# One PSUM pool for both forms of the first layer, a third chunk in float32, and the splits on GpSimd

## The chip, the cores and the metric

The kernel runs on one core of one Trainium2 chip. The metric is the device time of one execution in microseconds (us), lower is better. TensorE (PE in the profile; PEld is its weight load) multiplies matrices into PSUM, which has eight banks of 128 x 512 float32; VectorE (DVE), ScalarE (ACT) and GpSimd (POOL) work on elements, and GpSimd's operations here read and write SBUF alone; SyncE (SP) issues most DMA transfers.

## The reference

A Fourier mixing of 8 sequences of 3008 tokens of width 256, followed by a two-layer network with a hard-swish:

```python
X = np.fft.fft(x, axis=1)            # x: (8, 3008, 256) float32
X = np.fft.fft(X, axis=2).real       # bridge: (24064, 256)
h = X @ w_in                         # (256, 2048)
g = h * np.clip(h + 3.0, 0.0, 6.0) / 6.0
out = g @ w_out                      # (2048, 256)
```

## The kernel before

**Steps.** The batches are taken in four pairs p. Each pair has 12 chunks ck of 256 moving columns (the last is smaller), and each chunk goes through the 2048 hidden features in 8 blocks fc of 256. One (p, ck, fc) is a step s, 384 in all; a chunk is 8 steps. Below, "step 12" is s = 12, and "chunk 3" is the fourth chunk of the first pair, steps 24 to 31. The program runs with an order written out by hand: each engine takes its instructions in program order. In step s TensorE does the second layer for step s (`mlp2`, line 733, seven products per block, 14 matmul instructions of 256 columns; the float32 product is two instructions each) and the first layer for step s + 2.

**First layer, direct form** (`mlp1`, from `mlp1_products` and `activate`): tiles u and v are two float32 products (line 570, four instructions each); VectorE makes s (line 579), u (586) and v (588); ScalarE makes two relus (682); VectorE makes two gates (685), and these are the last readers of u's and v's banks. It is used for the steps below `SPLIT`, plus two, that is for chunks 0 and 1.

**First layer, split form** (`even_half`, `odd_half`, `other_sign`, `first_gate`, `second_gate`): u is still a float32 product (623), issued a step ahead; the product with the other half of the weights is made of six single-pass matmuls of a rounded type (639) from operands that are split in three parts: KW for the weights and k for the columns q. The split of KW is made once, by `split_w`, in four pieces of 512 columns in steps 8 to 11; k is made once per chunk by `split_q`. Both call `split` (605 on ScalarE, 607 and 608 on VectorE), and `split_w` adds two ScalarE scalings (615, 616). In each split-form step ScalarE copies tile y from v (644) ahead of the relu.

**Recombination.** GpSimd makes three sums per step (`combine`, line 699) that are the operands of four of the seven products; once per chunk, when its last block is done, it recombines the products (`finish`, in the first step of the next chunk), and VectorE transposes them for the store.

**Around the steps.** `beside(p)` puts work beside the steps: `ahead` runs at the start of a step, `middle_fns` in it, `behind` after the first part of `mlp2` (or inside `odd_half`). For the next pair of batches GpSimd loads and folds inputs (`load_x`, `fold`; for the second half of the first pair `load_half`, `fold_half`), TensorE does a first-stage unit (`stage1`, line 291; `stage1_quarters`, 395 and 398, in steps 8, 10, 15 and 18), whose two banks ScalarE copies out (302, 402), and a second stage (519, or 480 in steps 8, 16 and every 8 steps on), whose bank ScalarE copies into q (522, 483). Of the 24 units of `stage1`, eight belong to each later pair.

**PSUM.** Four banks hold the second layer's sums (`ps_a`). The other four are, up to step 13, pool `ps_d` (one bank, tag d) and pool `ps_h` (three banks in rotation, tag uv); in step 13 (`SPLIT - 1`) `close_ps` closes both and opens `ps_u` with four single banks a0, a1, y0 and y1. In the split form the step's parity picks the tags: u takes a, v takes y. A first-stage unit in step s takes y and a of parity s + 3; the even half of chunk step s + 3 comes right after part of `mlp2` and takes the same a. `stage1` copies first the y bank, then the a bank:

```python
ps = [bank([P, 2, D], "ps1"), other_bank([P, 2, D], "ps1")]
...
for b in range(2):
    nc.scalar.copy(z[:, b], ps[b][0:PB + PZ])
```

Of the kernel before, what the change touches and what calls it, by code (L numbers as in the profile page):

```python
# [60 lines left out]
def kernel(  # L61
# [10 lines left out]
    nc = tc.nc  # L72
# [38 lines left out]
    dctx = tc.tile_pool(name="ps_d", bufs=1, space=PSUM)  # L111
    ps_d = dctx.__enter__()
    hctx = tc.tile_pool(name="ps_h", bufs=3, space=PSUM)
    ps_h = hctx.__enter__()
    ps_u = None

    x_r = x.rearrange("b (r n) d -> (b r) (n d)", n=XC)
    x_pn = x.rearrange("b (n1 n2) d -> (b n1) n2 d", n2=N2)
# [151 lines left out]
    def bank(shape, name):  # L270
        if starting[0]:
            return ps_a.tile(shape, F32, tag="acc", name=name)
        if ps_u is not None:
            return ps_u.tile(shape, F32, tag=f"y{turn_of[0] % 2}", name=name)
        return ps_d.tile(shape, F32, tag="d", name=name)

    def other_bank(shape, name):
        if ps_u is not None:
            return ps_u.tile(shape, F32, tag=f"a{turn_of[0] % 2}", name=name)
        return ps_h.tile(shape, F32, tag="uv", name=name)  # L280

    def stage1(pr, c):
        y = pr.y[c]
        ps = [bank([P, 2, D], "ps1"), other_bank([P, 2, D], "ps1")]
        for h in range(2):
            last = (c, h) == (NXC - 1, 1)
            for b in range(2):
                n = 1 if last else 2  # L290
                nc.tensor.matmul(ps[b][h * PB:(h + 1) * PB, 0:n], F[rows(b), 0:PB], y[rows(b), 2 * h:2 * h + n],  # L291
                                 start=True, stop=not last, skip_group_check=last)


            cosine, sine = slice(0, P + 1), slice(P + 1, D)
            for k, (j, cs) in enumerate([(XC - 1, cosine), (XC, cosine), (XC - 1, sine), (XC, sine)] if last else ()):
                for b in range(2):
                    nc.tensor.matmul(ps[b][h * PB:(h + 1) * PB, 1, cs], table(k + 1, b), y[rows(b), j, cs],
                                     start=False, stop=(k % 2 == 1), skip_group_check=True)
        z = zpool.tile([PB + PZ, 2, 2, D], F32, tag="z", name="z")  # L300
        for b in range(2):
            nc.scalar.copy(z[:, b], ps[b][0:PB + PZ])  # L302
# [17 lines left out]

    def first_banks(m):
        if not middle:
            middle.extend(ps_h.tile([P, NM, 2, 1], F32, tag="uv", name="pt") for h in range(2))
        return [bank([P, 2, D], "ps1") for h in range(2)], [t[:, m] for t in middle]

    def quarters(m, part):
# [59 lines left out]
    def stage1_quarters(hb, m):  # L386
# [14 lines left out]
        for h in range(2):  # L401
            nc.scalar.copy(z[:, h], ps[h][0:PX])
# [156 lines left out]

    def mlp1_products(ch, fc, between=None):  # L560
        of, nq, q = ch.ck % 2 * TB, ch.nq, ch.pr.q[ch.ck // 2]
        u = ps_h.tile([P, 2, TB], F32, tag="uv", name="u")
        v = ps_h.tile([P, 2, TB], F32, tag="uv", name="v")
        for blk, ps in ((0, u), (1, v)):
            if blk and between:
                between()
            r = slice(0, P - blk)
            for i in range(2):
                f = 2 * fc + i
                nc.tensor.matmul(ps[:, i, 0:nq], W1[r, blk, f * P:(f + 1) * P], q[r, blk, of:of + nq],  # L570
                                 start=True, stop=True)
        return u, v

    def activate(ch, fc, u, v, between=None):
        of, nq, qn = ch.ck % 2 * TB, ch.nq, ch.pr.qn[ch.ck // 2]
        s = spool.tile([P, 2, TB], F32, tag="s", name="s")
        for i in range(2):
            f = 2 * fc + i
            nc.vector.scalar_tensor_tensor(s[:, i, 0:nq], qn[:, of:of + nq], WN[:, f:f + 1], u[:, i, 0:nq],  # L579
                                           op0=AL.mult, op1=AL.add)  # L580
# [5 lines left out]
        nc.vector.scalar_tensor_tensor(u[:], s[:], 1.0, v[:], op0=AL.mult, op1=AL.add)  # L586
        relu(t[:, 0], u[:], 1.0 / 6.0)
        nc.vector.scalar_tensor_tensor(v[:], s[:], -1.0, v[:], op0=AL.mult, op1=AL.add)
# [15 lines left out]
    def split(high, low, rest, x):  # L604
        nc.scalar.mul(high, x, 1.0 - EPS / 2.0)
        h = high.bitcast(F32)
        nc.vector.tensor_tensor(low, x, h, op=AL.subtract)
        nc.vector.scalar_tensor_tensor(rest, h, 1.0 + EPS, x, op0=AL.mult, op1=AL.subtract)

    def split_w(i):  # L610

        cs = slice(i * WB, (i + 1) * WB)
        low, rest = (spool.tile([P, WB], F32, tag="s", name="part") for j in range(2))
        split(KW[:, 0, cs], low[:], rest[:], W1[:, 1, cs])
        nc.scalar.mul(KW[:, 1, cs], low[:], 1.0 / EPS)
        nc.scalar.mul(KW[:, 2, cs], rest[:], -1.0 / EPS)
# [16 lines left out]
    def odd_half(ch, fc, step, between):  # L633
# [8 lines left out]
        t = spool.tile([P, 2, 2, TB], F32, tag="t", name="t")  # L642
        un, vn, yn, tn = u[:, :, 0:nq], v[:, :, 0:nq], y[:, :, 0:nq], t[:, :, :, 0:nq]
        nc.scalar.copy(yn, vn)  # L644
        between()
        nc.vector.scalar_tensor_tensor(un, un, 1.0 + EPS, yn, op0=AL.mult, op1=AL.add)  # L646
        relu(tn[:, 0], un, 1.0 / 6.0)
        ch.front[fc] = [u, v, t, s]

    def other_sign(ch, fc):  # L650
# [196 lines left out]
    def exponent_b(j):  # L847
        pm = [PM[j % len(PM)][:, i].bitcast(F16) for i in range(2)]
        if j in (0, 1, 4):
            exs[j] = ps_h.tile([P, WB], F32, tag="uv", name="ex")[:]  # L850
        elif j in (2, 5):
            exs[j] = ps_d.tile([P, WB], F32, tag="d", name="ex")[:]
        elif j % 2 == 0:
            exs[j] = bank([P, WB], "ex")[:]
        else:
# [80 lines left out]
        nc.sync.dma_start(out=F[:, 0:5 * PB], in_=c_stage1[:, 8 * PB:13 * PB])  # L936

    def keep_awake(n, w=2 * TB):
        ps = ps_d.tile([P, 2 * TB], F32, tag="d", name="awake")
# [6 lines left out]
    awake = ps_d.tile([P, TB // 4], F32, tag="d", name="awake")  # L946
# [133 lines left out]
    def beside(p):  # L1080
# [72 lines left out]
    def close_ps():  # L1153
        nonlocal ps_u
        hctx.__exit__(None, None, None)
        dctx.__exit__(None, None, None)
        ps_u = ctx.enter_context(tc.tile_pool(name="ps_u", bufs=1, space=PSUM))
# [103 lines left out]
    def run(fns, t):  # L1261
        for f, a in fns.get(t, ()):
            f(*a)

    prev = None
    for s, (p, ck, fc) in enumerate(steps):
        if ck == 0 and fc == 0:
# [12 lines left out]
        else:  # L1280
# [9 lines left out]
            if s < SPLIT:  # L1290
                run(middle_fns, t)
                mlp1(*chunk(s + 2))
                if s == SPLIT - 1:
                    close_ps()
                    split_q(chunk(s + 3)[0])
                    even_half(*chunk(s + 3), s + 3)
                make_combine()
                mlp2(*chunk(s), 0)
                run(behind, t)
                mlp2(*chunk(s), 1)  # L1300
            else:
# [12 lines left out]
                mlp2(*chunk(s), 1, 1 + (t in behind))  # L1314
# [107 lines left out]
```

## Time and profile before

| | |
|---|---|
| median of 3 runs | 1901.78 us (1900.34 to 1902.53) |
| the profiled execution | 1902.44 us, span 1900.4 us |
| mean granted clock of TensorE in it | 0.997 |
| busy: TensorE, VectorE, GpSimd, ScalarE | 99%, 79%, 77%, 49% |

A line of the timeline has the start in us, the busy time in us, the engine, the line of the kernel, the operation, output <- inputs, shapes, how many instructions were merged, and in brackets the idle time before it with what ended it. A line of a group has the total busy time in us, the mean of one instruction in ns, and the idle time before. A line of a table of waits has the waiting engine and line, what it waited for, the total in us, how often, and the longest. Matmul ends are modelled, so that lengths of matmul groups are best read from start to start.

### The profile page before, as it was taken

How to read it: one execution, taken by the hardware profiler on the slowest of the kernel's cores; microseconds unless marked ns; L12 is line 12 of the kernel's file. 1: busy time of each engine (PE TensorE's matmuls, PEld its weight loads, DVE VectorE, ACT ScalarE, POOL GpSimd, SP SyncE). 2: the span in 40 equal slices, each digit the busy share in tenths (PEclk: the TensorE clock that was granted, in tenths of full speed). 3: DMA queues.
4: the chain of work that ended last, by engine and by line, in shares of the span. 5: the costliest groups of instructions: out<-in, count | busy, mean ns of one | idle time of the engine just before them, and what ended most of it. 6: DMA issues, size and time to landing. Idle time of an engine off the chain costs nothing.

```text
span 1900.4 us, 30550 instructions
## 1 busy us (share of the span) xinstructions
PE 1873.6 (99%) x10192; PEld 1642.0 (86%) x10192; DVE 1505.1 (79%) x2856; ACT 931.4 (49%) x1591; POOL 1457.0 (77%) x1658
## 2 busy tenths in 40 slices
PE   9989999999999999999999999999999999999998
PEld 6668888888988888888998888888899898999988
DVE  8977777777887777777887777777778887887887
ACT  6545444445445444454454444544454444444443
POOL 5676889887778887888768878888767667666775
PEclk9989999999999999999999999999999999999999
DMA  7432233311112223221112221222101101111011
GB/s 266 109 92 59 70 75 104 87 48 47 48 32 68 56 64 79 54 67 36 40 39 57 66 69 45 67 56 61 48 23 35 42 14 38 37 26 40 17 23 21
DMA packets 157378, 110.40 MB, mean 58 GB/s; under 512 B 122095, under 2 KB 135898, under 8 KB 157222
## 3 DMA queue, kind: packets, MB, share of 16 engines
q1 hardware_dynamic: 144966, 71.24, 14.9%
q0 software_dynamic: 11008, 36.63, 6.7%
q8 instruction: 81, 1.33, 0.3%
q10 hardware_dynamic: 1248, 0.59, 0.1%
q14 instruction: 75, 0.61, 0.1%
HBM read 71.93 MB, written 36.79 MB: 57 GB/s over the span
## 4 chain that ended last, share of the span: by engine, by line
PE 91%; DVE 4%; ACT 2%; issue 2%; POOL 1%; DMA 0%; DVEq 0%; ACTq 0%; POOLq 0%
PE acc L733 55%; PE u L623 16%; PE u L639 9%; PE v L639 4%; PE ps L519 2%; PE ps L291 1%; ACT z L302 1%; DVE a L685 1%; ACT t L682 1%; PE acc L709 1%; DVE s L579 0%; DVE s L629 0%; DVE u L586 0%; PE ps L356 0%; PE v L570 0%
## 5 line engine op out<-in xcount | busy, mean ns | idle before, releaser
L699 POOL TENSOR_TENSOR c<-a 128x512 f32<-128x512 f32 (+1 forms) x375 | 473.1, 1262 | 322.7 <-DVE a L685 269.8
L733 PE MATMUL acc<-c,G 128*128 128x256 f32 (+1 forms) x3008 | 701.0, 376 | 0.4 <-POOL c L699 0.2
L733 PEld LDWEIGHTS acc<-c,G 128*128 128x128 f32 x3008 | 566.6, 191 | 75.3 <-POOL c L699 3.4
L733 PE MATMUL acc<-a,G 128*128 128x256 f32 (+1 forms) x2256 | 603.6, 377 | 0.0
L733 PEld LDWEIGHTS acc<-a,G 128*128 128x128 f32 x2256 | 395.5, 190 | 53.8 <-issue 15.9
L629 DVE SCALAR_TENSOR_TENSOR s<-qn,WS,u 128x256 f32<-128x256 f32 (+1 forms) x736 | 315.9, 470 | 156.3 <-PE u L623 156.0
L682 ACT ACTIVATE t<-v,half 128x512 f32<-128x512 f32 (+1 forms) x384 | 260.7, 679 | 353.3 <-DVE v L653 350.2
L682 ACT ACTIVATE t<-u,half 128x512 f32<-128x512 f32 (+1 forms) x384 | 260.1, 677 | 353.5 <-DVE u L646 321.8
L623 PE MATMUL u<-q,W 128*128 128x256 f32 (+1 forms) x1472 | 374.3, 377 | 6.3 <-DVE a L685 3.1
L646 DVE SCALAR_TENSOR_TENSOR u<-u,y 128x512 f32<-128x512 f32 (+1 forms) x368 | 250.4, 680 | 154.8 <-ACT y L644 152.3
L623 PEld LDWEIGHTS u<-q,W 128*128 128x128 f32 x1472 | 274.2, 190 | 52.2 <-ACT z L302 12.3
L685 DVE SCALAR_TENSOR_TENSOR a<-t,v 128x512 f32<-128x512 f32 (+1 forms) x480 | 265.9, 571 | 57.9 <-ACT t L682 55.6
L644 ACT COPY y<-v 128x512 f32<-128x512 f32 (+1 forms) x368 | 213.7, 581 | 176.6 <-PE v L639 174.9
L699 POOL TENSOR_TENSOR c<-c,a 128x256 f32<-128x256 f32 (+1 forms) x375 | 271.9, 725 | 29.4
L699 POOL TENSOR_TENSOR c<-a,c 128x256 f32<-128x256 f32 (+1 forms) x375 | 270.5, 721 | 29.4
L685 DVE SCALAR_TENSOR_TENSOR a<-t,u 128x512 f32<-128x512 f32 (+2 forms) x448 | 261.3, 595 | 2.9 <-ACT t L682 2.9
L653 DVE SCALAR_TENSOR_TENSOR v<-s,u 128x512 f32<-128x512 f32 (+1 forms) x368 | 250.0, 679 | 1.3 <-ACT t L682 0.7
L639 PE MATMUL u<-k,KW 128*128 128x256 f32 (+1 forms) x1472 | 231.6, 279 | 1.8 <-DVE s L629 1.8
L639 PE MATMUL v<-k,KW 128*128 128x256 f32 (+1 forms) x736 | 214.0, 372 | 0.0
L639 PEld LDWEIGHTS u<-k,KW 128*128 128x128 f32 x1472 | 198.4, 188 | 2.4 <-ACT t L682 2.4
L639 PEld LDWEIGHTS v<-k,KW 128*128 128x128 f32 x736 | 139.0, 190 | 17.5
L699 POOL TENSOR_TENSOR r<-w,e 128x256 f32<-128x256 f32 (+1 forms) x92 | 88.9, 987 | 3.6
(147 smaller groups left out, 1179.0 us busy)
## 6 DMA issues: line engine op xcount, KB each, us to landing
out_dram<-o SPq DMA_DIRECT2D x744, 32.0 KB
T<-in_c_stage_dram SPq DMA_DIRECT2D x26, 512.0 KB
g<-zd SPq DMA_DIRECT2D x42, 256.0 KB
zd<-z SPq DMA_DIRECT2D x48, 192.0 KB
xt<-in_x_dram POOLq DMA_DIRECT2D x21, 256.0 KB
qn<-qd SPq DMA_DIRECT2D x16, 256.0 KB
st<-in_moe_w_out_dram POOLq DMA_DIRECT2D x7, 512.0 KB
xt<-in_x_dram POOLq DMA_DIRECT2D x17, 192.0 KB
```

The costliest lines, as they stand in the source:

```text
L291: nc.tensor.matmul(ps[b][h * PB:(h + 1) * PB, 0:n], F[rows(b), 0:PB], y[rows(b), 2 * h:2 * h + n], start=True, stop=not last, skip_group_c ...
L519: nc.tensor.matmul(ps[:, blk, u * P:n].rearrange("p (b k) -> p b k", b=2), g[:, kk, blk * (P + 1):blk * (P + 1) + P], T[gr][:, :, blk, kk, ...
L623: nc.tensor.matmul(u[:, i, 0:nq], W1[:, 0, f * P:(f + 1) * P], q[:, 0, of:of + nq], start=(i == 0), stop=True, skip_group_check=True)
L629: nc.vector.scalar_tensor_tensor(s[:, i, 0:nq], qn[:, of:of + nq], WS1[:, f:f + 1], u[:, i, 0:nq], op0=AL.mult, op1=AL.add)
L639: nc.tensor.matmul(o[:, i, 0:nq], KW[:, j, fs], ch.k[:, j, 0:nq], start=(j == 2 and i == 0), stop=True, skip_group_check=True)
L644: nc.scalar.copy(yn, vn)
L646: nc.vector.scalar_tensor_tensor(un, un, 1.0 + EPS, yn, op0=AL.mult, op1=AL.add)
L653: nc.vector.scalar_tensor_tensor(vn, sn, -2.0 * (1.0 + EPS), un, op0=AL.mult, op1=AL.add)
L682: nc.scalar.activation(t, h, AF.Relu, bias=half[:], scale=scale)
L685: nc.vector.scalar_tensor_tensor(dst, t, 1.0, h, op0=AL.min, op1=AL.mult)
L699: (eng or nc.gpsimd).tensor_tensor(out, in0, in1, op=AL.add)
L733: nc.tensor.matmul(ch.acc[i // 2][:, i % 2, 0:ch.n], G[:, i, fc, :], mv, start=(fc == 0 and i % 2 == 0), stop=(fc == NF - 1), skip_group_c ...
```

## The change

1. `ps_u` is opened at the beginning with its four tags, and no pool is closed. Up to the switch, a0 stands for the former `ps_d` (`lone_tile`), and a1, y0 and y1 are taken in rotation for the former `ps_h` (`ring_tile`).
2. `SPLIT` goes from 14 to 22: chunk 2 has the direct form too (its s uses the scaled row WS1, and `back` undoes the scale), and the split form begins with chunk 3. At the switch, three products of `mlp2` come ahead of `odd_half`.
3. `split_w` makes eight pieces of 256 columns, one in every second step from 8 to 22. In `split` VectorE's two operations become two of GpSimd and one of ScalarE; the pieces have a tag of their own.
4. `split_q` is called at the end of the step five steps ahead of its chunk, not four, and goes through the same `split`.
5. `stage1` and `stage1_quarters` copy the a bank (`ps[1]`) first, then hand back control (`yield`); in `odd_half` the VectorE operation on u and the relu are issued there, and only then the copy of the y bank with the transfers that follow it.

```diff
+    ps_u = ctx.enter_context(tc.tile_pool(name="ps_u", bufs=1, space=PSUM))
+    RING = ("a1", "y0", "y1")
+    ring = [0]
+
+    def ring_tile(shape, name):
+        ring[0] += 1
+        return ps_u.tile(shape, F32, tag=RING[(ring[0] - 1) % 3], name=name)
+
+    def lone_tile(shape, name):
+        return ps_u.tile(shape, F32, tag="a0", name=name)
...
         z = zpool.tile([PB + PZ, 2, 2, D], F32, tag="z", name="z")
-        for b in range(2):
-            nc.scalar.copy(z[:, b], ps[b][0:PB + PZ])
+        nc.scalar.copy(z[:, 1], ps[1][0:PB + PZ])
+        yield
+        nc.scalar.copy(z[:, 0], ps[0][0:PB + PZ])
...
         of, nq, qn = ch.ck % 2 * TB, ch.nq, ch.pr.qn[ch.ck // 2]
+        wn, back = (WN, 1.0) if ch.ck < 2 else (WS1, 1.0 + EPS)
...
     def split(high, low, rest, x):
         nc.scalar.mul(high, x, 1.0 - EPS / 2.0)
         h = high.bitcast(F32)
-        nc.vector.tensor_tensor(low, x, h, op=AL.subtract)
-        nc.vector.scalar_tensor_tensor(rest, h, 1.0 + EPS, x, op0=AL.mult, op1=AL.subtract)
+        nc.gpsimd.tensor_tensor(low, x, h, op=AL.subtract)
+        nc.scalar.mul(rest, h, EPS)
+        nc.gpsimd.tensor_tensor(rest, rest, low, op=AL.subtract)

     def split_w(i):

-        cs = slice(i * WB, (i + 1) * WB)
-        low, rest = (spool.tile([P, WB], F32, tag="s", name="part") for j in range(2))
+        cs = slice(i * TB, (i + 1) * TB)
+        low, rest = (spool.tile([P, TB], F32, tag="part", name="part") for j in range(2))
         split(KW[:, 0, cs], low[:], rest[:], W1[:, 1, cs])
         nc.scalar.mul(KW[:, 1, cs], low[:], 1.0 / EPS)
         nc.scalar.mul(KW[:, 2, cs], rest[:], -1.0 / EPS)
...
         nc.scalar.copy(yn, vn)
-        between()
+        late = between()
         nc.vector.scalar_tensor_tensor(un, un, 1.0 + EPS, yn, op0=AL.mult, op1=AL.add)
         relu(tn[:, 0], un, 1.0 / 6.0)
+        finish_parts(late)
...
-            for i in range(FF // WB):
-                put(NF + i, split_w, i)
+            for i in range(NF):
+                put(NF + 2 * i, split_w, i)
...
-    SPLIT = 2 * NF - 2
+    SPLIT = 3 * NF - 2
...
             if s < SPLIT:
                 run(middle_fns, t)
                 mlp1(*chunk(s + 2))
-                if s == SPLIT - 1:
-                    close_ps()
-                    split_q(chunk(s + 3)[0])
-                    even_half(*chunk(s + 3), s + 3)
                 make_combine()
                 mlp2(*chunk(s), 0)
-                run(behind, t)
+                if s == SPLIT - 1:
+                    even_half(*chunk(s + 3), s + 3)
+                finish_parts(begin_parts(t))
                 mlp2(*chunk(s), 1)
             else:
                 turn_of[0] = s + 3
+                n = 3 if s == SPLIT else 1 + (t in behind)
+                if s == SPLIT:
+                    mlp2(*chunk(s), 0, n)
                 if s + 2 < len(steps):
-                    odd_half(*chunk(s + 2), s + 2, lambda: run(behind, t))
-                mlp2(*chunk(s), 0, 1 + (t in behind))
+                    odd_half(*chunk(s + 2), s + 2, lambda: begin_parts(t))
+                if s > SPLIT:
+                    mlp2(*chunk(s), 0, n)
...
-                if s + 4 < len(steps) and (s + 4) % NF == 0:
-                    split_q(chunk(s + 4)[0])
+            if s > SPLIT - 6 and s + 5 < len(steps) and (s + 5) % NF == 0:
+                split_q(chunk(s + 5)[0])
```

More of the change, by code (lines that the diff above doesn't have):

```diff
@@ L110 @@
     ps_a = ctx.enter_context(tc.tile_pool(name="ps_a", bufs=4, space=PSUM))
[L111 to L115, printed above, removed]
+    ps_u = ctx.enter_context(tc.tile_pool(name="ps_u", bufs=1, space=PSUM))
[6 more added lines that the diff above has]
+        return ps_u.tile(shape, F32, tag="a0", name=name)
     x_r = x.rearrange("b (r n) d -> (b r) (n d)", n=XC)
@@ L272, in bank @@
             return ps_a.tile(shape, F32, tag="acc", name=name)
-        if ps_u is not None:
+        if turn_of[0]:
             return ps_u.tile(shape, F32, tag=f"y{turn_of[0] % 2}", name=name)
-        return ps_d.tile(shape, F32, tag="d", name=name)
+        return lone_tile(shape, name)
     def other_bank(shape, name):
-        if ps_u is not None:
+        if turn_of[0]:
             return ps_u.tile(shape, F32, tag=f"a{turn_of[0] % 2}", name=name)
-        return ps_h.tile(shape, F32, tag="uv", name=name)
+        return ring_tile(shape, name)
     def stage1(pr, c):
@@ L322, in first_banks @@
         if not middle:
-            middle.extend(ps_h.tile([P, NM, 2, 1], F32, tag="uv", name="pt") for h in range(2))
+            middle.extend(ring_tile([P, NM, 2, 1], "pt") for h in range(2))
         return [bank([P, 2, D], "ps1") for h in range(2)], [t[:, m] for t in middle]
@@ L400, in stage1_quarters @@
         z = zpool.tile([PX, 2, 2, D], F32, tag="z", name="z")
-        for h in range(2):
-            nc.scalar.copy(z[:, h], ps[h][0:PX])
+        nc.scalar.copy(z[:, 1], ps[1][0:PX])
+        yield
+        nc.scalar.copy(z[:, 0], ps[0][0:PX])
         zc = zpool.tile([PX, 2, 2], F32, tag="zc", bufs=4, name="zc")
@@ L561, in mlp1_products @@
         of, nq, q = ch.ck % 2 * TB, ch.nq, ch.pr.q[ch.ck // 2]
-        u = ps_h.tile([P, 2, TB], F32, tag="uv", name="u")
-        v = ps_h.tile([P, 2, TB], F32, tag="uv", name="v")
+        u = ring_tile([P, 2, TB], "u")
+        v = ring_tile([P, 2, TB], "v")
         for blk, ps in ((0, u), (1, v)):
@@ L578, in activate @@
             f = 2 * fc + i
-            nc.vector.scalar_tensor_tensor(s[:, i, 0:nq], qn[:, of:of + nq], WN[:, f:f + 1], u[:, i, 0:nq],
+            nc.vector.scalar_tensor_tensor(s[:, i, 0:nq], qn[:, of:of + nq], wn[:, f:f + 1], u[:, i, 0:nq],
                                            op0=AL.mult, op1=AL.add)
@@ L585, in activate @@
         ch.a[fc] = a
-        nc.vector.scalar_tensor_tensor(u[:], s[:], 1.0, v[:], op0=AL.mult, op1=AL.add)
+        nc.vector.scalar_tensor_tensor(u[:], s[:], back, v[:], op0=AL.mult, op1=AL.add)
         relu(t[:, 0], u[:], 1.0 / 6.0)
-        nc.vector.scalar_tensor_tensor(v[:], s[:], -1.0, v[:], op0=AL.mult, op1=AL.add)
+        nc.vector.scalar_tensor_tensor(v[:], s[:], -back, v[:], op0=AL.mult, op1=AL.add)
         relu(t[:, 1], v[:], -1.0 / 6.0)
@@ L849, in exponent_b @@
         if j in (0, 1, 4):
-            exs[j] = ps_h.tile([P, WB], F32, tag="uv", name="ex")[:]
+            exs[j] = ring_tile([P, WB], "ex")[:]
         elif j in (2, 5):
-            exs[j] = ps_d.tile([P, WB], F32, tag="d", name="ex")[:]
+            exs[j] = lone_tile([P, WB], "ex")[:]
         elif j % 2 == 0:
@@ L938, in keep_awake @@
     def keep_awake(n, w=2 * TB):
-        ps = ps_d.tile([P, 2 * TB], F32, tag="d", name="awake")
+        ps = lone_tile([P, 2 * TB], "awake")
         for i in range(n):
@@ L945 @@
     nc.vector.memset(ones[:], 1.0)
-    awake = ps_d.tile([P, TB // 4], F32, tag="d", name="awake")
+    awake = lone_tile([P, TB // 4], "awake")
     for i in range(56):
@@ L1151, in close_w @@
         KW = ctx.enter_context(tc.tile_pool(name="kpool", bufs=1)).tile([P, 3, FF], F32R, name="KW")
[L1153 to L1157, printed above, removed]
     epool = KW = None
     steps = [(p, ck, fc) for p in range(NP) for ck in range(NCK) for fc in range(NF)]
-    SPLIT = 2 * NF - 2
+    SPLIT = 3 * NF - 2
     def chunk(s):
@@ L1263, in run, with begin_parts, finish_parts @@
             f(*a)
+    def begin_parts(t):
+        parts = [f(*a) for f, a in behind.get(t, ())]
+        for part in parts:
+            next(part)
+        return parts
+    def finish_parts(parts):
+        for part in parts:
+            next(part, None)
     prev = None
@@ L1313 @@
                 make_combine()
-                mlp2(*chunk(s), 1, 1 + (t in behind))
-                if s + 4 < len(steps) and (s + 4) % NF == 0:
-                    split_q(chunk(s + 4)[0])
+                mlp2(*chunk(s), 1, n)
+            if s > SPLIT - 6 and s + 5 < len(steps) and (s + 5) % NF == 0:
+                split_q(chunk(s + 5)[0])
         if fc == NF - 1:
```

## The prediction

> **What bounds the kernel now.** I read the page first (span, busy times, slices), then TensorE's timeline around the place where the form of the first layer switches, then VectorE's, ScalarE's and GpSimd's timelines of the same stretch, then TensorE's waits over the rest.
>
> ```profile
> span 1900.4 us, 30550 instructions
> ...
> PE 1873.6 (99%) x10192; PEld 1642.0 (86%) x10192; DVE 1505.1 (79%) x2856; ACT 931.4 (49%) x1591; POOL 1457.0 (77%) x1658
> ```
>
> TensorE is busy 99%: a change pays only by taking matmul passes away, or idle time and slow-clock time on TensorE. The starts of the split form's first matmul (L639, tile v) are the kernel's clock:
>
> ```profile
> 137.30 0.58 PE L639 MATMUL v<-k,KW 128*128 128x256 f32 x2
> ...
> 141.89 0.59 PE L639 MATMUL v<-k,KW 128*128 128x256 f32 x2
> ...
> 148.08 0.58 PE L639 MATMUL v<-k,KW 128*128 128x256 f32 x2
> ...
> 178.10 0.58 PE L639 MATMUL v<-k,KW 128*128 128x256 f32 x2
> ```
>
> 137.30 to 141.89 is a plain step of the split form: 4.59 us. The next one, 6.19 us, carries one unit of the first stage, so such a unit costs 1.60. The switch itself is not clean:
>
> ```profile
> 92.36 1.03 PE L570 MATMUL u<-q,W 128*128 128x256 f32 x4
> ...
> 96.80 1.08 PE L395 MATMUL ps<-y,F 47*64 47x512 f32 x8 [1.25 <-POOL G L901]
> ...
> 98.27 3.41 PE L733 MATMUL acc<-c,G 128*128 128x256 f32 x8
> ...
> 116.09 1.89 PE L733 MATMUL acc<-c,G 128*128 128x256 f32 x8
> 117.82 1.03 PE L570 MATMUL u<-q,W 128*128 128x256 f32 x4
> 121.16 1.13 PE L570 MATMUL v<-q,W 127*128 127x256 f32 x4 [2.32 <-DVE a L685]
> ...
> 124.24 2.76 PE L733 MATMUL acc<-c,G 128*128 128x256 f32 x8
> 126.84 1.03 PE L570 MATMUL u<-q,W 128*128 128x256 f32 x4
> 127.70 1.03 PE L570 MATMUL v<-q,W 127*128 127x256 f32 x4
> ...
> 131.81 1.13 PE L623 MATMUL u<-q,W 128*128 128x256 f32 x4 [3.08 <-DVE a L685]
> ```
>
> Eight passes of the second layer take 1.73 us from 116.09 to 117.82, 0.216 each. Three waits stand in brackets, and after each the same eight passes are slow (3.41, 2.76). The windows give the clock (columns: each engine's busy time, then PEclk):
>
> ```profile
> 99.00:101.00 2.00, 2.00 (x6) 1.60 (x5) 0.76 (x2) 1.33 (x3) 1.84 (x3) 0.50 0.94 358
> ...
> 123.00:125.00 2.00, 2.00 (x6) 1.64 (x5) 1.77 (x4) 1.34 (x2) 1.57 (x3) 0.50 0.21 52
> ```
>
> The granted clock is 0.50 some 2 us after an idle time of 1.25 or 2.32 us. The price, from 98.27: 3.41 for passes worth 1.73, so about 1.7 us on top of the wait. [...]
>
> **Part 1, the switch moved by eight steps, with one PSUM pool.** Why those waits:
>
> ```profile
> 114.62 2.25 DVE L607 TENSOR_TENSOR part<-W,KW 128x512 f32<-128x512 f32 x1 [0.44 <-ACT KW L605]
> 116.79 1.21 DVE L608 SCALAR_TENSOR_TENSOR part<-KW,W 128x512 f32<-128x512 f32 x1
> ...
> 96.14 0.56 ACT L483 COPY q<-ps 128x512 f32<-128x512 f32 x1
> ...
> 116.90 0.63 ACT L615 ACTIVATE KW<-part 128x512 fp32r<-128x512 f32 x1 [2.31 <-DVE part L607]
> ```
>
> The last weight piece held VectorE for 3.4 us (114.62 to 117.92, where step 12's first operation could begin), and the gates that give back u's and v's banks came late: the 2.32. The 3.08 is the closing of the two old pools: the new pool's first tile waited for the last gate of the old ones. The change takes VectorE out of the weight pieces and closes no pool, so both reasons go. The 1.25 is put down to GpSimd, but ends with the copy that ends at 96.70 and gives back the bank, queued on ScalarE behind a weight piece. It stays, with a shorter piece: I take 0.7 and, as no wait of this size is followed by a low clock later in the trace (0.7 at most, waits below), no clock loss.
>
> What TensorE must do from 92.36 (step 8) to the point that before reaches at 178.10 (step 22 begins, the even half of chunk 3 done) is, in the direct form: 14 steps of 22 passes at 0.216, 66.6; four first-stage units, 1.47 for the first (96.80 to 98.27) and 1.09 for three others (an estimate: the row at 96.80, 1.08), 4.7; one second-stage half, 8 passes of half width, and one even half, 4 passes, 0.9 each by the same 0.216. Sum 73.1 against 85.74 (178.10 less 92.36). So 12.6 us are there to be won; the direct form's price, 0.17 a step over 4.59, is inside.
>
> What is late next is GpSimd, with ScalarE behind it. Each of eight pieces gives GpSimd two operations of 128x256, and two of ScalarE's four wait for them.
>
> ```profile
> L699 POOL TENSOR_TENSOR c<-c,a 128x256 f32<-128x256 f32 x344 | 253.4, 736 | 27.0
> ...
> 110.35 1.26 POOL L223 TENSOR_TENSOR xt<-xt 111x508 f32<-111x508 f32 x1
> ...
> 115.03 1.27 POOL L699 TENSOR_TENSOR c<-a 128x512 f32<-128x512 f32 x1
> ...
> 118.55 1.25 POOL L229 TENSOR_TENSOR y<-xt 111x508 f32<-111x508 f32 x1
> ...
> 152.21 0.73 POOL L699 TENSOR_TENSOR r<-e 128x256 f32<-128x256 f32 x1
> ...
> 156.98 1.28 POOL L699 TENSOR_TENSOR c<-a 128x512 f32<-128x512 f32 x1
> ```
>
> A pair costs 2 x 0.74 plus gaps, 1.6. In step 11 GpSimd works from 110.35 to 118.55 (fold, two gathers, combine), 8.2 us in a step of 4.76. Now the pair of step 12 stands behind that. TensorE, rid of its waits, begins step 12 at 92.36 + 4 x 4.76 + 1.47 + 1.09 + 0.7 = 114.7. ScalarE reaches the piece before step 12's relu, waits for GpSimd's 118.5 and 119.3, and is free at about 120.5 (its copies are half of 0.63 and some fixed part). The relu was due at 117.3 (u done at 115.6, then three VectorE operations, about 1.7, an estimate from 0.68 for one of 128x512); relu and gate take 0.68 each, so the gate that frees u ends near 122.0, while TensorE asks for that bank at 114.7 + 4.76 + 0.87 = 120.3. **A wait of 1.7, and by the rows above 1.7 of slow clock.** The same comes once more: the recombination of chunk 1 (152.21 to 156.98, 4.8 us) is queued in step 16 with a pair, another pair follows in step 18: again 1.7 + 1.7, and 0.6 of short waits around it. With the 0.7 of step 8 that is 8.1. **Part 1: 12.6 - 8.1 = 4.5 gained.** Bounds: 12.6 if the pairs hide, -4 if each pair takes twice the row. [...]
>
> **Part 2, u's bank first.** After the switch a first-stage unit writes two banks; the even half then asks for the one of tag a.
>
> ```profile
> 227.99 1.13 PE L733 MATMUL acc<-a,G 128*128 128x256 f32 x4
> 228.11 1.07 ACT L302 COPY z<-ps 112x512 f32<-112x512 f32 x2
> ...
> 229.24 0.73 PEld L623 LDWEIGHTS u<-q,W 128*128 128x128 f32 x4 [0.52 <-ACT z L302]
> ...
> PEld u L623 <- ACT z L302: 12.3, 24, 0.5
> ```
>
> The bank in question is copied second, so the weight load waits until 229.18. TensorE's four passes from 227.99 end at 228.86 (4 x 0.216); the matmul starts at 229.24 at the earliest: 0.38 lost, and about 0.1 more as the load could not run ahead. Copied first, the bank is free at 228.65, before 228.86. VectorE's next operation is not behind the copies, the relu moves ahead of the second copy, and that copy's bank (tag y) is asked for a step later, so nothing new waits. 24 units x 0.46 = **11.0 gained**; bounds 24 x 0.33 and 24 x 0.51, so 8 to 12.3. The two units of chunk 1 that moved into the direct form are in part 1.
>
> **Part 3, q split by GpSimd, a step earlier.** VectorE's share of this collides with GpSimd:
>
> ```profile
> 211.74 2.65 DVE L607 TENSOR_TENSOR k<-q,k 128x256 fp32r<-128x256 f32 x1
> ...
> 215.69 0.58 PE L639 MATMUL v<-k,KW 128*128 128x256 f32 x2
> ...
> 216.79 0.71 PE L639 MATMUL u<-k,KW 128*128 128x256 f32 x4 [0.52 <-DVE s L629]
> ...
> 221.40 0.58 PE L639 MATMUL v<-k,KW 128*128 128x256 f32 x2
> ...
> PE u L639 <- DVE s L629: 1.8, 3, 0.7
> ...
> PE ps L291 <- DVE a L685: 2.0, 4, 0.7
> ...
> PEld acc L733 <- POOL c L699: 2.6, 6, 0.6
> ```
>
> The step from 215.69 to 221.40 is 1.12 longer than 4.59. There are three such waits, 3 x 1.12 = 3.4; of the four waits of the first stage on VectorE I count two behind a split, 1.4. **4.8 gained** (3.4 to 5.4). Against it, 1.6 us of GpSimd per chunk. A plain step leaves GpSimd 4.59 less a combine of 1.28 + 0.74 + 0.74 and gaps, about 1.75 us, and it runs a step ahead; only in the first pair of batches, where a fold or a load comes every second or third step, is it late now (the last row, at most 2.6 us). Counting a backlog there with folds of 2.4 and 2.7, I find one more overrun, near step 37, of 1.4: **1.5 lost** (0 to 4). ScalarE's two multiplications there wait for nobody, so no relu is held.
>
> **Sum.** 4.5 + 11.0 + 4.8 - 1.5 = 18.8. The profiled execution took 1902.44 (its span 1900.4), the median of the runs shown is 1901.78, 0.66 below. 1902.44 - 18.8 - 0.66 = 1883.0.
>
> **The rivals.** *The switch goes clean* (GpSimd is ahead, ScalarE is never held): 8.1 more, 1874.9. For it speaks that GpSimd has idle stretches there now; against it that TensorE's own waits made them. 0.14.
>
> [...] 0.10. [...]
>
> *The bank order wins nothing*, because ScalarE reaches the first copy late: 1883.0 + 11.0 = 1894.0. The copy at 228.11 starts as the unit's matmuls end, which speaks against it. 0.06.
>
> *Slower*: every weight piece holds ScalarE until TensorE waits. Eight times 3 us of wait and 1.7 of slow clock are 37.6 in place of 8.1: 1912.5. Break-even is 26.9 us of such loss (8.1 + 18.8), 3.4 a piece; as a piece's first 1.6 are largely hidden, that takes a pair of some 4 us, over twice the row. A write in the rounded type, which no GpSimd row shows, might do it for q. 0.10. The two rivals before this one together give 1901.8, no change: 0.03.
>
> **Chances and range.** Forecast 0.57, rivals 0.14, 0.10, 0.06, 0.10, 0.03. About 0.2% (4 us) is what a measurement of this kernel can tell from no change. Faster 0.87, same 0.03, slower 0.10. The range from 1873 to 1894 takes in the clean switch and the two weaker gains and leaves the last two cases and the tails out; the forecast's own is 1876 to 1890.
>
> **What would show it.** Steps with a first-stage unit at 5.7 instead of 6.19, and no wait of L623's loads on z. No L570 wait over 2.4 between 92 and 170; waits of about 1.7 on gates in steps 13 and 18 or 19, each followed by PEclk 0.50. VectorE without splits, GpSimd's pair at 1.6. No step of 5.7 without a unit or a second-stage half. It is wrong if ScalarE's weight copies wait over 3 us for GpSimd in most pieces, or if first-stage steps stay at 6.19.

## The result, and the profile after

| | us |
|---|---|
| before, median of the runs beside it | 1901.16 (1899.61 to 1902.53) |
| changed kernel, median of 5 | 1881.22 (1880.64 to 1881.55) |
| ratio | 0.9895, 95% interval 0.988 to 0.9909 |
| profiled execution | 1880.88, span 1879.1 |

The forecast was 1883.0 with a range of 1873 to 1894. The page of the changed kernel, first lines:

```profile
span 1879.1 us, 30498 instructions
...
PE 1861.5 (99%) x10176; PEld 1639.5 (87%) x10176; DVE 1421.0 (76%) x2756; ACT 949.6 (51%) x1647; POOL 1523.3 (81%) x1764
```

VectorE lost 84 us of work and GpSimd gained 66; TensorE, the bound, is busy 12 us less and idle 9 us less. In the changed file the lines are a little further down: L577 is the direct form (570 before), L632 the split form's u (623), L648 its rounded products (639), L743 the second layer (733), L296 the first stage (291), L692 and L695 relu and gate (682, 685), L709 the combine (699).

TensorE's timeline of the changed kernel around the switch:

```profile
92.93 1.03 PE L577 MATMUL u<-q,W 128*128 128x256 f32 x4
...
96.46 1.08 PE L401 MATMUL ps<-y,F 47*64 47x512 f32 x8 [0.34 <-issue]
...
121.81 1.13 PE L577 MATMUL v<-q,W 127*128 127x256 f32 x4 [0.80 <-DVE a L695]
...
144.17 1.13 PE L577 MATMUL v<-q,W 127*128 127x256 f32 x4 [0.68 <-DVE a L695]
...
155.53 1.13 PE L577 MATMUL u<-q,W 128*128 128x256 f32 x4 [1.24 <-DVE a L695]
...
158.66 1.89 PE L743 MATMUL acc<-c,G 128*128 128x256 f32 x8
160.39 1.03 PE L577 MATMUL u<-q,W 128*128 128x256 f32 x4
...
170.76 1.46 PE L743 MATMUL acc<-a,G 128*128 128x256 f32 x6
```

From step 8 (92.93) to the start of step 22 (170.76) it takes 77.83 us, where before took 85.74: **7.9 gained**. The brackets hold what is left of waiting, 3.06 us, in steps 8, 13, 17 and 19. After the wait of 1.24 eight passes take 1.73 (158.66 to 160.39): no slow clock. Here are TensorE's windows of that place (third column from the right: granted clock):

```profile
154.00:156.00 2.00, 0.76 (x4) 0.44 (x3) 1.21 (x3) 2.00 (x5) 1.84 (x3) 1.00 0.63 99
156.00:158.00 2.00, 2.00 (x11) 1.75 (x10) 1.89 (x6) 0.60 (x2) 1.92 (x3) 1.00 0.48 193
```

A step with a first-stage unit, in the timeline of the changed kernel:

```profile
562.42 0.59 PE L648 MATMUL v<-k,KW 128*128 128x256 f32 x2
...
564.43 1.13 PE L743 MATMUL acc<-a,G 128*128 128x256 f32 x4
564.56 0.59 ACT L306 COPY z<-ps 112x512 f32<-112x512 f32 x1 [0.82 <-PE ps L296]
565.05 0.69 ACT L692 ACTIVATE t<-u,half 128x512 f32<-128x512 f32 x1
565.20 0.82 PEld L632 LDWEIGHTS u<-q,W 128*128 128x128 f32 x4
565.39 1.03 PE L632 MATMUL u<-q,W 128*128 128x256 f32 x4
...
568.23 0.59 PE L648 MATMUL v<-k,KW 128*128 128x256 f32 x2
```

The a bank's copy (L306) is over at 565.15 and the weight load starts at 565.20; the step takes 5.81 us (562.42 to 568.23) instead of 6.19. In 19 of the 24 such steps the gain is 0.37 to 0.39. In four steps that carry a second-stage half as well it is 0.27, and in step 32 nothing, for a reason that the waits over the rest of the trace show (TensorE first, then its weight loads):

```profile
PE ps L296 <- DVE a L695: 0.7, 2, 0.3
PE acc L743 <- POOL c L709: 0.2, 1, 0.2
PE ps L487 <- ACT z L308: 0.2, 1, 0.2
...
PEld acc L743 <- POOL c L709: 2.6, 6, 0.6
...
PEld ps L526 <- ACT z L308: 1.0, 4, 0.3
PEld ps L487 <- ACT z L308: 0.6, 1, 0.6
```

The waits of u's loads on z (12.3 us before) are gone; new are five waits of the second stage for the y bank, whose copy (L308) now stands behind the relu. 19 x 0.38 + 4 x 0.27 - 0.08 = **8.2 gained**. The waits of u L639 on VectorE's s (1.8, three times) are gone too, and those of the first stage on gates fell from 2.0 to 0.7: seven steps that stood behind a split by VectorE are 1.12, 0.16, 0.17, 1.25, 0.68, 1.28 and 0.74 shorter, **5.4 gained**. The waits for GpSimd's c are 2.6 us, six times, as before. 7.9 + 8.2 + 5.4 = 21.5, less a start of step 8 that is 0.57 later, is 20.9 of the 21.3 by which the spans differ.

### The profile page after: what moved, and what is told of

Read it like the earlier page. It is cut to its first block, busy times and chain, and to the rows that moved or that the text cites. A ratio compares the mean times of both kernels' runs of the same rounds, so it can differ in the third digit from the quotient of the medians.

```text
span 1879.1 us, 30498 instructions
## 1 busy us (share of the span) xinstructions
PE 1861.5 (99%) x10176; PEld 1639.5 (87%) x10176; DVE 1421.0 (76%) x2756; ACT 949.6 (51%) x1647; POOL 1523.3 (81%) x1764
## 4 chain that ended last, share of the span: by engine, by line
PE 91%; DVE 3%; POOL 2%; issue 1%; ACT 1%; DMA 1%; SPq 0%; DVEq 0%; POOLq 0%; ACTq 0%
PE acc L743 57%; PE u L632 16%; PE u L648 9%; PE v L648 4%; PE ps L526 2%; PE ps L296 1%; POOL c L709 1%; DVE a L695 1%; PE v L577 1%; PE acc L719 1%; ACT t L692 1%; PE u L577 1%; POOL xt L188 0%; DVE top L882 0%; DVE s L587 0%
## 5 line engine op out<-in xcount | busy, mean ns | idle before, releaser
L743 PE MATMUL acc<-c,G 128*128 128x256 f32 (+1 forms) x3008 | 698.6, 375 | 0.4 <-POOL c L709 0.2
L743 PEld LDWEIGHTS acc<-c,G 128*128 128x128 f32 x3008 | 564.4, 190 | 76.1 <-POOL c L709 4.5
L709 POOL TENSOR_TENSOR c<-a 128x512 f32<-128x512 f32 (+1 forms) x375 | 470.8, 1255 | 193.8 <-DVE a L695 165.6
L743 PE MATMUL acc<-a,G 128*128 128x256 f32 (+1 forms) x2256 | 599.7, 376 | 0.0
L692 ACT ACTIVATE t<-v,half 128x512 f32<-128x512 f32 (+1 forms) x384 | 261.0, 680 | 356.4 <-DVE v L663 355.0
L743 PEld LDWEIGHTS acc<-a,G 128*128 128x128 f32 x2256 | 395.2, 190 | 52.3 <-issue 14.3
L638 DVE SCALAR_TENSOR_TENSOR s<-qn,WS,u 128x256 f32<-128x256 f32 (+1 forms) x720 | 309.4, 471 | 162.2 <-PE u L632 161.2
L692 ACT ACTIVATE t<-u,half 128x512 f32<-128x512 f32 (+1 forms) x384 | 260.8, 679 | 300.1 <-DVE u L655 262.3
L655 DVE SCALAR_TENSOR_TENSOR u<-u,y 128x512 f32<-128x512 f32 (+1 forms) x360 | 245.4, 682 | 193.6 <-ACT y L653 190.5
L632 PE MATMUL u<-q,W 128*128 128x256 f32 (+1 forms) x1440 | 362.8, 374 | 0.0
L695 DVE SCALAR_TENSOR_TENSOR a<-t,v 128x512 f32<-128x512 f32 (+1 forms) x480 | 265.7, 570 | 57.3 <-ACT t L692 54.9
L632 PEld LDWEIGHTS u<-q,W 128*128 128x128 f32 x1440 | 270.5, 190 | 34.6
L653 ACT COPY y<-v 128x512 f32<-128x512 f32 (+1 forms) x360 | 208.6, 580 | 174.4 <-PE v L648 172.7
L709 POOL TENSOR_TENSOR c<-a,c 128x256 f32<-128x256 f32 (+1 forms) x375 | 269.5, 719 | 29.4
L709 POOL TENSOR_TENSOR c<-c,a 128x256 f32<-128x256 f32 (+1 forms) x375 | 269.5, 719 | 29.4
L695 DVE SCALAR_TENSOR_TENSOR a<-t,u 128x512 f32<-128x512 f32 (+2 forms) x448 | 261.0, 594 | 15.4 <-ACT t L692 15.4
L663 DVE SCALAR_TENSOR_TENSOR v<-s,u 128x512 f32<-128x512 f32 (+1 forms) x360 | 243.7, 677 | 0.9 <-ACT t L692 0.7
L648 PE MATMUL u<-k,KW 128*128 128x256 f32 (+1 forms) x1440 | 226.1, 279 | 0.0
L648 PE MATMUL v<-k,KW 128*128 128x256 f32 (+1 forms) x720 | 208.7, 371 | 0.0
L648 PEld LDWEIGHTS u<-k,KW 128*128 128x128 f32 x1440 | 193.7, 188 | 0.0
L648 PEld LDWEIGHTS v<-k,KW 128*128 128x128 f32 x720 | 136.0, 190 | 17.1
L709 POOL TENSOR_TENSOR r<-w,e 128x256 f32<-128x256 f32 (+1 forms) x92 | 88.9, 988 | 3.6
```

What stands on the lines that cost most here:

```text
L632: nc.tensor.matmul(u[:, i, 0:nq], W1[:, 0, f * P:(f + 1) * P], q[:, 0, of:of + nq], start=(i == 0), stop=True, skip_group_check=True)
L648: nc.tensor.matmul(o[:, i, 0:nq], KW[:, j, fs], ch.k[:, j, 0:nq], start=(j == 2 and i == 0), stop=True, skip_group_check=True)
L663: nc.vector.scalar_tensor_tensor(vn, sn, -2.0 * (1.0 + EPS), un, op0=AL.mult, op1=AL.add)
L692: nc.scalar.activation(t, h, AF.Relu, bias=half[:], scale=scale)
L695: nc.vector.scalar_tensor_tensor(dst, t, 1.0, h, op0=AL.min, op1=AL.mult)
L709: (eng or nc.gpsimd).tensor_tensor(out, in0, in1, op=AL.add)
```

## The experiments

The kernels of one group ran beside runs of the kernel before of 1901.18 (**old_order**, **new_order_relu_behind**, **q_on_vector**, **before_new_order**), 1900.80 (**w_on_vector**, **switch_at_14**, **q_a_step_later**, **scale_later**) and 1901.65 us (the other three). Differences are against the changed kernel's 1881.22 unless said otherwise. The interval of a ratio reaches about 0.17% to each side, some 3 us; smaller differences between two of these kernels rest on the waits and step lengths in the traces, not on the times.

**old_order** undoes the order of the banks (here and in the next two, the same edit in `stage1_quarters` is left out of the diff):

```diff
-        nc.scalar.copy(z[:, 1], ps[1][0:PB + PZ])
-        yield
         nc.scalar.copy(z[:, 0], ps[0][0:PB + PZ])
+        nc.scalar.copy(z[:, 1], ps[1][0:PB + PZ])
+        yield
```

> The changed kernel, but a first-stage unit's two banks are copied in the old order (y bank, then a bank), both ahead of the VectorE operation on u and the relu. Theory (the even half waits for the a bank): units after the switch go back from 5.81 to 6.19 us a step, 24 x 0.38 = 9.1, so about 1881.2 + 9 = 1890, and 24 waits of L632's weight loads on z of 0.5 us return. Rival (the gain came from the relu or from VectorE's freedom): under 3 us of difference.

Measured: 1888.28, ratio to before 0.9933 (0.9917 to 0.995), 7.1 slower (8.1 by the spans of the profiled executions). Its units are back at 6.19 us, and the row of waits is the old one:

```profile
PEld u L632 <- ACT z L307: 12.3, 24, 0.5
```

So the bank's wait is the mechanism of these units. It is 8.1 and not the 9.1 expected because the change gains less than 0.38 in the five steps with a second-stage half.

**new_order_relu_behind** keeps the a bank first, but issues both copies ahead of the relu:

```diff
         nc.scalar.copy(z[:, 1], ps[1][0:PB + PZ])
-        yield
         nc.scalar.copy(z[:, 0], ps[0][0:PB + PZ])
+        yield
```

> The changed kernel, a bank copied first, but both copies ahead of the relu (no yield between them). Theory (only the order of the two banks counts): steps with a unit stay at 5.81, time within 1 us of 1881.2. The second-stage banks that waited 0.1 to 0.3 us for the late y copy (steps 32, 131, 167, 227, 263) get it earlier, up to 1 us gained. Rival (the relu's place makes the gain): back to 1890.

Measured: 1879.18, ratio 0.9892 (0.9875 to 0.9908), 2.0 faster than the change by the medians (1878.67 to 1881.70 against 1880.64 to 1881.55, which overlap). All plain units cost 5.81, and the waits of the second stage on z are gone: step 32 takes 6.69 instead of 7.16, the four others with a second-stage half are 0.11 shorter. So the relu's place gains nothing, and lets the second stage wait for the y bank: 0.9 us. The other 1.1 lies ahead of step 8 (its first unit begins at 95.26, in the changed kernel at 96.46), where no edit is; this start differs by up to 1.2 us between the profiled executions here, and its cause is open.

**before_new_order** is the kernel before with nothing but the order of the two copies changed:

```diff
-        for b in range(2):
+        for b in (1, 0):
             nc.scalar.copy(z[:, b], ps[b][0:PB + PZ])
```

> The kernel before with one edit: the a bank is copied ahead of the y bank, nothing else. Theory: 24 units x 0.38, and two units of chunk 1 in the split form, together 9.9: 1901.2 - 9.9 = 1891.3, the waits of L623's weight loads on z gone. Rival (order alone does little while the relu stands behind both copies): over 1897.

Measured: 1891.32, ratio 0.9955 (0.9938 to 0.9971), 9.9 faster than the kernel before, to the tenth what was expected; part of that is luck. The units give 24 x 0.38 = 9.1, and step 46 loses 1.08 of it again (5.69 us instead of 4.60). The rest comes from the switch: steps 8 to 13 take 42.46 us (92.31 to 134.77) instead of 44.94 (92.36 to 137.30). There the timeline has the three waits of the kernel before, one of 1.18 where that had 0.29, and a surprise:

```profile
96.76 1.08 PE L395 MATMUL ps<-y,F 47*64 47x512 f32 x8 [1.26 <-POOL G L901]
...
112.12 1.13 PE L570 MATMUL u<-q,W 128*128 128x256 f32 x4 [1.18 <-DVE a L685]
...
120.32 1.13 PE L570 MATMUL v<-q,W 127*128 127x256 f32 x4 [2.32 <-DVE a L685]
121.29 1.46 PE L733 MATMUL acc<-a,G 128*128 128x256 f32 x6
122.59 1.89 PE L733 MATMUL acc<-c,G 128*128 128x256 f32 x8
124.31 1.03 PE L570 MATMUL u<-q,W 128*128 128x256 f32 x4
125.18 1.03 PE L570 MATMUL v<-q,W 127*128 127x256 f32 x4
129.28 1.21 PE L623 MATMUL u<-q,W 128*128 128x256 f32 x4 [3.08 <-DVE a L685]
130.28 2.77 PE L733 MATMUL acc<-a,G 128*128 128x256 f32 x6
```

After the wait of 2.32 the passes are at full speed (1.72 for eight, 122.59 to 124.31; granted clock 1.00 from 121 to 125); only the 3.08 is followed by a low clock (0.50 from 131 to 133). In the kernel before all three were, by 0.50.

**q_on_vector**, **q_a_step_later** and **q_on_vector_a_step_later** are the other corners of part 3: the engine of q's split, and its place.

```diff
-        split(k[:, 0, 0:nq], k[:, 1, 0:nq], k[:, 2, 0:nq], q[:, of:of + nq])
+        high, x = k[:, 0, 0:nq], q[:, of:of + nq]
+        nc.scalar.mul(high, x, 1.0 - EPS / 2.0)
+        h = high.bitcast(F32)
+        nc.vector.tensor_tensor(k[:, 1, 0:nq], x, h, op=AL.subtract)
+        nc.vector.scalar_tensor_tensor(k[:, 2, 0:nq], h, 1.0 + EPS, x, op0=AL.mult, op1=AL.subtract)
```

> The changed kernel, but the two element operations of q's split are VectorE's again, at the new place (five steps ahead). Theory (VectorE's operation with two SBUF operands is held while GpSimd works): three or more of them stretch beyond 2 us, with TensorE waits after them, 3 to 6 us slower, 1884 to 1887. Rival (the place, a step earlier, made the gain): no stretch that TensorE sees, within 1 us of 1881.2.

```diff
-            if s > SPLIT - 6 and s + 5 < len(steps) and (s + 5) % NF == 0:
-                split_q(chunk(s + 5)[0])
+            if s > SPLIT - 5 and s + 4 < len(steps) and (s + 4) % NF == 0:
+                split_q(chunk(s + 4)[0])
```

> The changed kernel with q's split on GpSimd, but at its old place, four steps ahead of its chunk. Theory (the engine alone matters): within 1 us of 1881.2, steps with a wait after a split as few as now. Rival (the place matters too, since the split on VectorE at the new place brought back only about 2.5 of the 5.4 us): 2 to 3 us slower, with late sums (TensorE's loads of c on GpSimd) near the splits.

> The changed kernel with q's split back on VectorE and at its old place, four steps ahead: the fourth corner beside the changed kernel, q_on_vector and q_a_step_later. Theory (the two act together: VectorE's operations stretch beside GpSimd at either place, but at the old one folds stand beside more of them): about 5 us slower than the changed kernel, 1886, with three steps of 5.7 to 5.9 again. Rival (VectorE costs the same at both places): 1883.7 as q_on_vector.

| | five steps ahead | four steps ahead |
|---|---|---|
| GpSimd | 1881.22 | 1880.61 (0.9895, 0.9879 to 0.9912) |
| VectorE | 1883.67 (0.9916, 0.9898 to 0.9934) | 1886.91 (0.992, 0.9903 to 0.9937) |

On GpSimd the place costs nothing; on VectorE it does. At the old place three steps of 5.67 to 5.86 are back, and with them the rows of the kernel before:

```profile
PE ps L296 <- DVE a L699: 2.0, 4, 0.7
PE u L652 <- DVE s L642: 1.8, 3, 0.7
```

At the new place TensorE loses 0.74 and 0.75 in steps 109 and 205, and 0.56, 0.67 and 0.56 in steps 93, 189 and 285; both the 2.5 in time and the count of operations over 2 us, two, are below what was expected. Why: VectorE's two operations, by line, at the new place and then the first one in the changed kernel on GpSimd (duration in ns: least, median, most):

```profile
L613 DVE TENSOR_TENSOR k<-q,k x45: 353/418/2293, 160.3 to 1831.3; 128x256 fp32r<-128x256 f32 x41, 128x194 fp32r<-128x194 f32 x4
L614 DVE SCALAR_TENSOR_TENSOR k<-k,q x45: 411/1487/1512, 160.7 to 1831.6; 128x256 fp32r<-128x256 f32 x41, 128x194 fp32r<-128x194 f32 x4
```

```profile
L615 POOL TENSOR_TENSOR k<-q,k x45: 599/731/745, 160.1 to 1827.6; 128x256 fp32r<-128x256 f32 x41, 128x194 fp32r<-128x194 f32 x4
```

VectorE's first operation is faster than GpSimd's by the median (418 against 731) and slower by the worst case (2293 against 745); its second takes 1487 in the median, GpSimd's (L617) 729. The two worst cases stand ahead of steps 109 and 205. Steps 93, 189 and 285 follow splits without such a case (418 at most and 1218 at most): they are steps of the pair's smaller last chunk, 3.81 us in the changed kernel, and there, as the other steps show no such loss, the ordinary length of the split seems to be enough.

**w_on_vector** puts the weight pieces back on VectorE, cut and spread as in the change:

```diff
-        split(KW[:, 0, cs], low[:], rest[:], W1[:, 1, cs])
+        high, x = KW[:, 0, cs], W1[:, 1, cs]
+        nc.scalar.mul(high, x, 1.0 - EPS / 2.0)
+        h = high.bitcast(F32)
+        nc.vector.tensor_tensor(low[:], x, h, op=AL.subtract)
+        nc.vector.scalar_tensor_tensor(rest[:], h, 1.0 + EPS, x, op0=AL.mult, op1=AL.subtract)
```

> The changed kernel, but the two element operations of each of the eight weight pieces are VectorE's (q's stay GpSimd's). Theory (VectorE with two SBUF operands is held while GpSimd works, and the gates stand behind it): some of the sixteen operations take over 1.5 us, waits of TensorE between steps 8 and 22 grow from 3.1 us to about 6, time 1884 to 1887. Rival (cutting the pieces in half and spreading them was enough): waits of 3.1 us or less, 1881 or below, as GpSimd is freed of 12.8 us there.

Measured: 1878.57, ratio 0.9884 (0.9868 to 0.9901), 2.7 *faster*: the rival held. The operations did stretch (by line: the first one of each piece, up to 1.80 us), but what TensorE waits for between steps 8 and 22 is 0.52 and 0.73 instead of 3.06:

```profile
L626 DVE TENSOR_TENSOR part<-W,KW x8: 416/908/1801, 93.1 to 167.4; 128x256 f32<-128x256 f32 x8
```

So the engine did not make the gain at the switch (0.75 of the 2.7 is an earlier step 8); on GpSimd the pieces stand behind its backlog and hold ScalarE (below). Smaller pieces, their spacing, the third chunk and the one pool are what is left. **switch_at_14** below takes back the chunk and the spacing; the size of the pieces and the pool were not tried alone.

**switch_at_14** puts the switch back to where it was, with a piece in each of steps 8 to 15:

```diff
-    SPLIT = 3 * NF - 2
+    SPLIT = 2 * NF - 2
-                put(NF + 2 * i, split_w, i)
+                put(NF + i, split_w, i)
```

> The changed kernel with the switch where it was before (chunk 2 in the split form) and the eight pieces one per step in steps 8 to 15. Theory (GpSimd's pairs need the room of the third direct chunk): 1.6 us more of GpSimd in each of these steps, ScalarE held longer in most of them, 3 to 6 us slower, 1884 to 1887, and any wait over 3 us lowers the clock as well. Rival (the third direct chunk buys nothing, the closing of the pools and VectorE's pieces were all): 8 x 0.17 = 1.4 faster, 1880.

Measured: 1888.19, ratio 0.9935 (0.9919 to 0.9952), 7.0 slower, more than the 3 to 6 expected. The longest of its waits, from TensorE's timeline, and the windows behind it:

```profile
126.67 1.70 PE L577 MATMUL v<-q,W 127*128 127x256 f32 x4 [3.22 <-DVE a L695]
```

```profile
128.00:130.00 2.00, 2.00 (x6) 1.55 (x6) 1.29 (x2) 0.00 (x0) 1.84 (x3) 0.50 0.00 0
```

From step 8 to the start of step 22 it takes 83.9 us there, against 77.83. The third chunk in float32 costs 1.4 us of matmul (8 steps of 0.17) and buys the room in which the pieces fit.

**scale_later** keeps the pieces on GpSimd, but issues ScalarE's two dependent copies a step later, behind the next relus:

```diff
-        nc.scalar.mul(KW[:, 1, cs], low[:], 1.0 / EPS)
-        nc.scalar.mul(KW[:, 2, cs], rest[:], -1.0 / EPS)
+        parts[i] = low, rest
...
+    def scale_w(i):
+        cs = slice(i * TB, (i + 1) * TB)
+        low, rest = parts.pop(i)
+        nc.scalar.mul(KW[:, 1, cs], low[:], 1.0 / EPS)
+        nc.scalar.mul(KW[:, 2, cs], rest[:], -1.0 / EPS)
...
                 put(NF + 2 * i, split_w, i)
+                put(NF + 2 * i + 1, scale_w, i)
```

> The changed kernel, but ScalarE's two scalings of a weight piece are issued one step later, behind the next relus, so that they wait for nothing. Theory (TensorE's waits in steps 13, 17 and 19 come from ScalarE, held by GpSimd's backlog ahead of the relu): the 0.80, 0.68 and 1.24 go, 2 to 3 us faster, 1878.5. Rival (GpSimd's backlog is itself the bound there): waits for c take their place, under 1 us gained.

Measured: 1878.17, ratio 0.9881 (0.9864 to 0.9897), 3.0 faster. Between steps 8 and 22 no wait on a gate is left; one for GpSimd's c, 0.84 us, took their place:

```profile
123.56 2.32 PE L750 MATMUL acc<-c,G 128*128 128x256 f32 x8 [0.84 <-POOL c L716]
```

**scale_later_relu_behind** joins the two edits that gained; **scale_later_relu_behind_three** adds a third product ahead of the even half in unit steps:

```diff
-                n = 3 if s == SPLIT else 1 + (t in behind)
+                n = 3 if s == SPLIT or t in behind else 1
```

> Two edits that each gained, together: ScalarE's scalings a step later (3.0 gained alone) and both copies of a first-stage unit ahead of the relu, a bank first (2.0 alone). They act at different steps, so theory: 1881.2 - 5.0 = 1876.2. Rival (the two share a wait): over 1877.5.

> As scale_later_relu_behind, and in a step with a first-stage unit three products of the second layer instead of two stand between the unit and the even half. Theory (of the 1.22 us that a unit still costs, 1.09 is matmul and the rest the end of the wait for the a bank): up to 24 x 0.13 = 3.1 more gained, 1873. Rival (the 0.13 is the unit's own, as its matmuls are of another shape): no difference to scale_later_relu_behind within 0.7 us, or slower if u's later product delays VectorE.

Measured: 1877.24, ratio 0.9869 (0.9851 to 0.9887), the fastest here together with 1877.16 (0.9867, 0.9849 to 0.9885) for the other. The first missed its 1876.2 by a microsecond: it has both mechanisms in its trace (no wait on gates at the switch, no second stage waiting for z), but of the 2.0 that were added for the relu's place only 0.9 belong to it. The third product does nothing: units stay at 5.81, and the 1873 that was hoped for was missed, so the 0.13 over the matmuls' 1.09 is not the bank's wait. What it is stays open.

## Why the prediction was right, point by point

The direction, the three parts and the places were as forecast; the sum was 18.8 against 21.5, of sizes that were off in both directions, so that the time came within 1.8 us of the forecast is in part luck.

**Part 1, 4.5 forecast, 7.9 measured.** The hold-up is the forecast one, at the forecast time. ScalarE's timeline of the changed kernel in step 12:

```profile
119.16 0.42 ACT L624 ACTIVATE KW<-part 128x256 fp32r<-128x256 f32 x1 [3.80 <-POOL part L615]
119.97 0.42 ACT L625 ACTIVATE KW<-part 128x256 fp32r<-128x256 f32 x1 [0.39 <-POOL part L617]
120.29 0.67 ACT L692 ACTIVATE t<-u,half 128x512 f32<-128x512 f32 x1
```

The relu starts at 120.29 (forecast 120.5), the wait falls on v in step 13, and the next ones in steps 17 and 19. ScalarE's weight copies waited over 3 us in two of the eight pieces (3.80 and 4.52), not in most of them. The terms of the 8.1 us were mis-sized: waits of 0.34, 0.80, 0.68 and 1.24 in place of 0.7, 1.7, 0.6 and 1.7 (v came about 0.6 later than reckoned, and the gate 0.3 earlier), and **3.4 us of slow clock that did not come**. That term was the failed step: it took two windows of one execution (0.50 in both) for a rule, and in before_new_order the waits of 1.26 and 2.32 cost no clock (1.00 after both). Without the term this part would have come to 12.6 - 4.7 = 7.9, which is what was measured.

That the two agree is luck. The waits came to 3.06 us and not to the 4.7 of that sum; without them the 14 steps took 74.8 us and not 73.1, in part because a unit costs 1.22 and not 1.09. The 7.9 itself hangs on the execution shown of the kernel before, which has three slow stretches: before_new_order, with one, passes steps 8 to 13 in 2.5 us less.

**Part 2, 11.0 forecast, 8.2 measured.** The rival that the bank order wins nothing is out (old_order, before_new_order). A unit went from 1.60 to 1.22, not to 1.14; 0.38 is the gain of the plain case. "Nothing new waits" was wrong for the five steps with a second-stage half, which takes the y bank within the same step. That cost 0.9 us, as new_order_relu_behind shows.

**Part 3, 4.8 gained and 1.5 lost forecast; 5.4 and nothing measured.** Seven steps stood behind splits, not five. The overrun near step 37 did not come: the waits for c are 2.6 us, six times, in both traces.

**The rivals.** The clean switch is what scale_later has, at 1878.2 and not 1874.9. The case of no change, 1901.8, took the splits on GpSimd to win nothing, and the bank order as well. For the splits half of that holds: for the weights the engine gained nothing in this kernel, with pieces small and apart (w_on_vector); for q it gains 2.5 to 6.3 us. What VectorE keeps did not slow down beside a busier GpSimd (81% instead of 77%), as this group of the kernel before and then of the changed kernel shows:

```profile
L653 DVE SCALAR_TENSOR_TENSOR v<-s,u 128x512 f32<-128x512 f32 (+1 forms) x368 | 250.0, 679 | 1.3 <-ACT t L682 0.7
```

```profile
L663 DVE SCALAR_TENSOR_TENSOR v<-s,u 128x512 f32<-128x512 f32 (+1 forms) x360 | 243.7, 677 | 0.9 <-ACT t L692 0.7
```

The rival on the slower side failed at its condition: a pair is 2 x 0.73, and a write in the rounded type costs no more (731 against 728 ns, medians of line 615).

## What to carry to other kernels

When an engine copies several PSUM banks out in a row, copy first the one that TensorE asks for next, and put no other work between the copies if a later stage of the same step asks for the last: the order of the two copies was worth 0.38 us in each plain unit, and 7.1 of this change's 20 us when it was taken back. Judge an operation moved between engines by its median and its worst duration beside the other engine's work, and by who queues behind it; a dependent operation that waits in an in-order queue is better issued a step later, behind the work that is due (3.0 us here, scale_later). Preparations for a change of form were cheaper here in small pieces far apart, though the slower form had to run a chunk longer.

## What the runs showed of the hardware

The granted clock does not follow from the length of a wait alone. In the kernel before, waits of 1.25, 2.32 and 3.08 us were each followed by 0.50; in before_new_order, with waits of 1.26, 2.32 and 3.08 at the same places, only the last was, and the others by 1.00; 1.24 in the changed kernel and two of 1.47 in switch_at_14 were followed by 1.00, 3.22 there by 0.50. So the three waits of 3.08 and 3.22 lowered the clock each time, and of the seven named from 1.24 to 2.32 two did. What decides between them stays open. In the windows of the kernel before (granted clock in the third column from the right) each slow stretch is 3.41 us long, with 1.00 in the 3.41 us ahead of it and behind it.

```profile
98.68:102.09 3.41, 3.41 (x10) 2.69 (x9) 2.17 (x3) 2.26 (x5) 3.25 (x4) 0.50 0.88 319
119.16:122.57 3.41, 1.41 (x7) 1.25 (x8) 3.10 (x6) 1.34 (x2) 2.77 (x4) 1.00 0.34 81
122.57:125.98 3.41, 3.41 (x10) 2.69 (x9) 2.58 (x4) 1.34 (x2) 2.43 (x4) 0.50 0.26 69
132.81:136.22 3.41, 3.41 (x10) 2.66 (x9) 1.50 (x3) 0.00 (x0) 3.25 (x5) 0.50 0.02 5
```

At half the clock such a stretch costs 1.7 us, the price that the prediction took. Their starts lie 23.89 and 10.24 us apart, 7.0 and 3.0 times that length; three starts do not show whether that is more than chance.

VectorE's operations with two SBUF operands took unlike times beside a working GpSimd. The first one of q's split has a median of 0.42 us and took up to 2.81 in the kernel before, 2.29 in q_on_vector and 2.81 in q_on_vector_a_step_later. The three over 2 us in the kernel before (at 211.74, 560.12 and 1019.62) had GpSimd at work almost without a break, but so had one of 0.42 (at 332.67). The second took 1.49 in the median, in q_on_vector 0.41 at least and 1.51 at most. What makes the difference these rows do not show. Those with one PSUM operand kept 0.68 in the mean (679 ns before, 677 in the changed kernel).
